# A norm by ScalarE's root, forms of one chunk made an expert later, and first products by pair of heads

## Chip, core and metric

The kernel runs on one core of one Trainium2 chip. The time is that of the whole program on the device, in microseconds (us); for this kernel the median of several executions is given. A core has five engines that run their own instruction streams in order and wait for each other by semaphores: TensorE (PE; its weight loads are listed apart as PEld), VectorE (DVE), ScalarE (ACT), GpSimd (POOL) and SyncE (SP), which here only issues DMA transfers. All data is float32.

## What is computed

Linear attention without softmax, normalised by its root mean square, followed by a mixture of four experts in which every token goes through every expert:

```python
# q, k, v: (8, 8, 576, 64); g_norm: (64,)
kv = np.einsum('bhsd,bhse->bhde', k, v)
out = np.einsum('bhsd,bhde->bhse', q, kv)
rms = np.sqrt(np.mean(out * out, axis=-1, keepdims=True) + 1e-06)
attn = out / rms * g_norm
x = attn.transpose(0, 2, 1, 3).reshape(4608, 512)
# domain_probs: (4608, 4); w1: (4, 512, 1024); w2: (4, 1024, 512)
p = domain_probs / (domain_probs.sum(-1, keepdims=True) + 1e-09)
for e in range(4):
    h = np.maximum(x @ w1[e], 0.0)
    out += p[:, e:e + 1] * (h @ w2[e])
```

## The kernel before

**Chunks.** The 4608 tokens are nine chunks of 512. Chunks 0 to 7 are the first 512 tokens of each batch element; chunk 8 holds the eight remainders of 64. The outer loop runs over the four experts, the inner one over the nine chunks; step s = 9e + c. Each step multiplies the chunk by w1 (`up`), applies relu, and multiplies by w2 (`down` or `down_deep`). Both products are made with fewer multiplications than usual: seven products of sums and differences of blocks (called forms, numbered 1 to 7, 12, 21) take the place of eight, and in `up` and `down_deep` this is done twice over, on quarters of blocks. The forms of the weights are made once for each expert (`weights_1`, `weights_2`), those of x once for each chunk (`x_forms`, in expert 0), stored to DRAM (`x_kept`), and loaded again for the later experts (`x_again`). Chunk 0 of expert 0 goes through `up_plain`, which needs no forms: eight output blocks i, each the sum of four products of a w1 block with x transposed, in two operations (dh = 0 and 1, each over two kt).

**Attention.** Batch element 0 is handled by `opening`, the others by `attention` in the steps of expert 0. In the opening each of four pairs of heads hp runs the same chain: `load_pair` issues loads of queries, keys and values (keys and values in 96 rows of 6 x 64 values, 1536 bytes in a run); `turn` transposes the queries on PE (L742); `key_values` multiplies keys by values (L761); `attend` multiplies queries by that (L788), into two PSUM banks `raw`; `scaled` squares on ACT (L640), sums on DVE (L647), computes (mean + 1e-6) to the power -0.5 on POOL in two instructions (L654, L658), and multiplies on DVE (L667); `turn_x` transposes on PE (L806), and ACT copies the result with the gains into half of x (L814; pairs 0 and 1 make the half xh[0], pairs 2 and 3 xh[1]). `attention` does the like for two pairs at once, with the power on POOL in L940 and L944, the multiply in L950 and the transposes in L1069.

**The order of the work** is made ahead by a planner (class `Plan`). Every operation has a key (steps of the program as a decimal number), estimated costs on the engines that may run it, the buffers that it reads and writes, and kinds of buffers with a fixed number of slots ("big" has 31, "xf" 5, PSUM banks "u1", "u2", "db", "ab" two each). The planner runs an event simulation with these costs: PE and SP take the first operation by key that is ready, the others the one that is due earliest, within a reach of about one key. An operation that names two engines (`either`) goes to DVE or POOL. The simulated order is the program order on every engine; estimates for transfers use the variables `bus` and `lanes`. While the first operation left on PE has a key under 0 and nothing is ready, the planner puts an `idle` operation on PE: two transposes of the identity into a free bank of "ab" or "db" (L1712), which compute nothing that is used. Operations marked `port` on DVE and POOL are kept from running at the same time by a dependency added at the end.

The helper `halves_of` records nearly all products (L410), `combine` all sums of forms (L433), `load` all loads (L439); one float32 matmul shows as two records on PE.

## Time and profile before

| | |
|---|---|
| median of 4 runs | 1666.7 us (1664.95 to 1668.14) |
| the profiled execution | 1665.69 us, span 1663.6 us |
| granted TensorE clock, mean | 0.999 |
| HBM read, written | 155.79 MB, 74.19 MB |

The span is from the first to the last instruction of the program. Times in the profile are from the span's start. Busy time of an engine is the union of its instructions; a matmul's end is modelled. Lines of the waits say which instruction's start waited for whom. A group's name such as `ab<-ident` is what the instruction writes and reads, by the program's names for buffers.

The stage that ends first is the opening with `up_plain` (about 0 to 60 us); the steps of expert 0 with attention go on to about 490 us, and each later step takes about 43 us.

| stretch, us | PE busy | DVE | ACT | POOL | DMA share, GB/s |
|---|---|---|---|---|---|
| 0 to 61.4 | 58.35 | 34.55 | 21.35 | 22.90 | 0.89, 221 |
| 150 to 194 (expert 0) | 44.00 | 34.40 | 25.35 | 26.75 | 0.69, 197 |
| 498 to 542 (expert 1, first step) | 44.00 | 36.26 | 29.14 | 25.21 | 0.67, 150 |
| 672 to 716 (expert 1) | 44.00 | 31.14 | 27.54 | 16.64 | 0.46, 112 |

### The profile page before, as it was taken

To read this page: it belongs to the slowest core of one execution; us is meant where nothing else is said; L and a number is where in the kernel's file an instruction comes from. 1 tells how busy PE (TensorE), PEld (TensorE's weight loads), DVE (VectorE), ACT (ScalarE), POOL (GpSimd) and SP (SyncE) were. 2 spreads that over 40 slices of the span, in tenths; PEclk is the share of its full clock that TensorE was granted. 3 is DMA by queue.
4 is the path that set the end of the run, shared out by engine and by line. 5 is a ranking of instruction groups with operands and counts; after the bars stand their busy time and mean duration, and the time that the engine had idled before them with its cause. 6 is when DMAs were issued, how large, how long until landed. Compare 5 with 4: busy or idle time off the path is not lost.

```text
span 1663.6 us, 66253 instructions
## 1 busy us (share of the span) xinstructions
PE 1651.4 (99%) x28884; PEld 1557.3 (94%) x28884; DVE 1250.8 (75%) x2051; ACT 972.8 (58%) x2391; POOL 705.0 (42%) x701
## 2 busy tenths in 40 slices
PE   9999999999999999999999999999999999999998
PEld 6587888888899999999999999999999999999996
DVE  4768777677788887776778777777788778777774
ACT  3355555555456666666666665656566566666662
POOL 3545443343445343333354554333355554333321
PEclk9999999999999999999999999999999999999999
DMA  9876765535456454444577444444579444444443
GB/s 220 196 224 189 214 177 148 143 124 182 149 172 147 125 121 114 113 109 115 144 177 177 116 119 114 110 109 116 133 179 200 116 116 116 104 115 116 116 104 52
DMA packets 208123, 234.27 MB, mean 141 GB/s; under 512 B 97368, under 2 KB 148440, under 8 KB 207832
## 3 DMA queue, kind: packets, MB, share of 16 engines
q1 hardware_dynamic: 184760, 193.32, 38.6%
q0 software_dynamic: 23072, 36.71, 15.5%
q8 instruction: 227, 3.72, 0.9%
q14 instruction: 64, 0.52, 0.1%
HBM read 155.79 MB, written 74.19 MB: 138 GB/s over the span
## 4 chain that ended last, share of the span: by engine, by line
PE 98%; DVE 1%; POOL 0%; DMA 0%; issue 0%; SPq 0%; ACT 0%; DVEq 0%; POOLq 0%; ACTq 0%
PE u L410 47%; PE db L410 32%; PE ab L410 15%; PE ab L1001 1%; PE ab L1069 1%; PE ab L1028 1%; PE ab L1712 1%; DMA big<-in_moe_w_dram 0%; DVE big L433 0%; PE ab L742 0%; POOL rt L944 0%; SPq L439 0%; PE ab L761 0%; PE ab L1090 0%; PE db L1037 0%
## 5 line engine op out<-in xcount | busy, mean ns | idle before, releaser
L433 DVE TENSOR_TENSOR big<-big,big 128x1024 f32<-128x1024 f32 (+1 forms) x527 | 518.7, 1001 | 35.7 <-ACT big L1226 15.9
L410 PE MATMUL u<-xf,big 128*64 128x128 f32 x6784 | 486.9, 273 | 0.2
L410 PEld LDWEIGHTS u<-xf,big 128*64 128x64 f32 x6784 | 394.0, 137 | 5.4 <-issue 1.0
L410 PE MATMUL u<-xf,w1y 128*64 128x128 f32 x5304 | 385.8, 273 | 0.0
L410 PE MATMUL db<-big,big 128*64 128x128 f32 (+1 forms) x4280 | 361.2, 308 | 1.3 <-ACT big L1576 0.4
L1270 DVE TENSOR_TENSOR big<-u,snap 128x256 f32<-128x256 f32 x476 | 199.5, 421 | 209.1 <-PE u L410 136.1
L433 POOL TENSOR_TENSOR big<-big,big 128x256 f32<-128x256 f32 (+1 forms) x196 | 219.1, 1135 | 224.6 <-DVE big L433 118.5
L410 PEld LDWEIGHTS u<-xf,w1y 128*64 128x64 f32 x5304 | 308.9, 137 | 2.4 <-issue 1.0
L410 PEld LDWEIGHTS db<-big,big 128*64 128x64 f32 x4280 | 262.3, 137 | 42.8 <-issue 2.8
L1262 ACT ACTIVATE snap<-u 128x256 f32<-128x256 f32 x490 | 188.2, 384 | 195.2 <-PE u L410 142.2
L1262 ACT ACTIVATE big<-u 128x256 f32<-128x256 f32 x476 | 181.7, 384 | 66.3 <-PE u L410 41.4
L1576 ACT ACTIVATE snap<-db 128x256 f32<-128x256 f32 (+1 forms) x230 | 82.4, 358 | 116.5 <-PE db L410 106.7
L1226 ACT ACTIVATE big<-big 128x1024 f32<-128x1024 f32 x134 | 140.7, 1050 | 5.6 <-DVE big L433 3.7
L433 POOL TENSOR_TENSOR big<-big 128x512 f32<-128x512 f32 (+1 forms) x76 | 94.4, 1250 | 114.9 <-DVE big L433 82.0
L410 PE MATMUL db<-small,big 128*64 128x128 f32 (+1 forms) x1552 | 116.9, 274 | 0.0
L1429 POOL DMA_DIRECT2D out_dram<-big x108 | 94.4, 1003 | 50.1 <-ACT big L1406 47.9
L1584 DVE TENSOR_TENSOR big<-ab,snap 128x256 f32<-128x256 f32 x166 | 69.9, 421 | 55.9 <-ACT snap L1576 30.0
L1262 ACT ACTIVATE u<-u 128x256 f32<-128x256 f32 x245 | 91.1, 372 | 24.5 <-PE u L410 9.1
L433 DVE TENSOR_TENSOR big<-big 128x512 f32<-128x512 f32 (+1 forms) x131 | 101.1, 784 | 1.8 <-PE u L410 1.7
L1614 POOL TENSOR_TENSOR big<-big 128x512 f32<-128x512 f32 x21 | 26.8, 1278 | 173.6 <-DVE big L433 140.9
L1406 ACT ACTIVATE big<-big,p_all 128x256 f32<-128x256 f32 x200 | 94.4, 501 | 5.4 <-POOL big L1614 4.0
L410 PEld LDWEIGHTS db<-small,big 128*64 128x64 f32 x1552 | 91.3, 137 | 0.7
(193 smaller groups left out, 2337.2 us busy)
## 6 DMA issues: line engine op xcount, KB each, us to landing
xf<-x SPq DMA_DIRECT2D x108, 512.0 KB, 3.7
out_dram<-big POOLq DMA_DIRECT2D x92, 256.0 KB, 5.5
xf<-x_h SPq DMA_DIRECT2D x81, 256.0 KB, 3.3
xf<-x SPq DMA_DIRECT2D x81, 256.0 KB, 3.7
x<-xf SPq DMA_DIRECT2D x36, 512.0 KB, 4.8
big<-in_moe_w_dram SPq DMA_DIRECT2D x32, 512.0 KB, 5.1
x_h<-big SPq DMA_DIRECT2D x18, 512.0 KB, 3.7
out_dram<-big SPq DMA_DIRECT2D x32, 256.0 KB, 3.6
```

The costliest lines, as they stand in the source:

```text
L410: nc.tensor.matmul(out_[cols], lhsT=lhsT[:, cols], rhs=rhs, **kw)
L433: lambda eng: adder(eng).tensor_tensor(out=out_(), in0=a(), in1=b(), op=op),
L1001: nc.tensor.matmul(bank.ap[r * D:(r + 1) * D, o * D:(o + 1) * D], lhsT=ks[r], rhs=vs[r], start=(j == 0), stop=(j == len(sets) - 1), skip_g ...
L1028: nc.tensor.matmul(raw[r].ap[c * D:(c + 1) * D, (o * NR + t) * D:(o * NR + t + 1) * D], lhsT=qt.ap[half, col:col + D], rhs=kv.ap[half, o * ...
L1226: lambda eng: nc.scalar.activation(out=b.ap[:], in_=b.ap[:], func=ACT.Relu),
L1262: lambda eng: nc.scalar.activation(out=where(), in_=ps.ap[:, 0:HN], func=ACT.Copy),
L1270: lambda eng: nc.vector.tensor_tensor(out=block(whole, a, t), in0=src.ap[:, 0:HN], in1=add_.ap[:], op=ALU.add),
L1406: lambda eng: nc.scalar.activation(out=cell(i, half), in_=ap(), func=ACT.Copy, scale=prob()),
L1429: nc.gpsimd.dma_start(out=dst, in_=cell(i)[parts, :], accum_op=ALU.add)
L1576: lambda eng: nc.scalar.activation(out=where(), in_=group_of(ps.ap), func=ACT.Copy),
L1584: lambda eng: nc.vector.tensor_tensor(out=cell(tq, dq), in0=group_of(src.ap), in1=group_of(add_.ap), op=ALU.add,),
L1614: lambda eng: adder(eng).tensor_tensor(out=whole(to), in0=whole(a), in1=whole(b), op=ALU.add),
```

## The change

Four things are changed, and some constants of the planner.

1. The power on POOL (`power`, in `scaled` and in `norm_rows` of `attention`) is replaced by `inverse_root`: ACT takes the square root of the mean plus epsilon, DVE takes its reciprocal r and makes one Newton step, r (1.5 - 0.5 a r r), with three more instructions.
2. The forms of chunk 0 are no longer made in expert 0. Only its two halves are stored. In expert 1 the chunk is taken fifth in place of first, and `x_first` loads its quarters, makes the forms and stores them for experts 2 and 3.
3. In `up_plain` a product is one operation for each pair of heads hp, which reads that pair's part of x (`x_part`), in place of one for each half. The first four blocks' products have keys under 0 for all four pairs. The opening's `raw` banks are halves of the two "db" banks for all pairs, so "u1" and "u2" stay free for the products; "db" is handed out when the opening's `raw` is done. The first block of w1 is loaded at key -2.85, behind the gains and before pair 2. The sums of w1's forms of expert 0 wait for the last norm of the opening (`after=opened`).
4. Keys and values are loaded in 72 rows of 8 x 64 values (2048 bytes in a run).

```diff
-        bus, port = 3.8, 0.0
+        bus, port = 2.5, 0.0
...
-                        bus = max(bus, t + 1.5) + op.kb / 215.0
-                        op.end = bus + 0.5
+                        bus = max(bus, t + 0.6) + op.kb / 215.0
+                        op.end = bus + 1.9
...
+    halved = slots["db"]
+    slots["raw"] = [[b[:, i * HN:(i + 1) * HN] for b in halved] for i in range(2)]
+    slots["db"] = []
     later = [
+        (("raw",), "db", halved),
...
-        return {"PE": passes * products * (0.0025 + columns / 1200.0) + 0.003}
+        return {"PE": passes * products * (0.0025 + columns / 1200.0)}
...
             load(
-                key + i * step, f[n],
+                key + i * step if e or i else -2.85, f[n],
                 lambda n=n: f[n].ap[:].rearrange("p (k u) -> p k u", k=2),
-                w1_src(e, dh, uh), 512 if e else 312, also=[corner[n]],
+                w1_src(e, dh, uh), 512 if e else 300, also=[corner[n]],
             )
...
-                [f[a], f[b], corner[a], corner[b]], [f[o], corner[o]],
+                [f[a], f[b], corner[a], corner[b]], [f[o], corner[o]], () if e else opened,
...
+    def inverse_root(key, ss, rt, n, count):
+
+        def root(eng):
+            nc.scalar.activation(
+                out=rt.ap[0:n, 0:count], in_=ss.ap[0:n, 0:count], func=ACT.Sqrt, scale=1.0 / D,
+                bias=eps[0:n, :],
+            )
+
+        def invert(eng):
+            a, r, w = ss.ap[0:n, 0:count], rt.ap[0:n, 0:count], rt.ap[0:n, 2 * H:2 * H + count]
+            nc.vector.reciprocal(out=r, in_=r)
+            nc.vector.scalar_tensor_tensor(
+                out=w, in0=a, scalar=D * EPS, in1=r, op0=ALU.add, op1=ALU.mult)
+            nc.vector.scalar_tensor_tensor(
+                out=w, in0=w, scalar=-0.5 / D, in1=r, op0=ALU.mult, op1=ALU.mult)
+            return nc.vector.scalar_tensor_tensor(
+                out=r, in0=w, scalar=1.5, in1=r, op0=ALU.add, op1=ALU.mult)
+
+        plan.add(key - 0.3, {"ACT": 0.2}, root, reads=[ss], writes=[rt])
+        plan.add(key - 0.3, {"DVE": 0.75}, invert, reads=[ss, rt], writes=[ss, rt], port=True)
...
-        plan.add(key - 0.3, {"POOL": 0.3 + 0.37 * blocks}, power, reads=[ss], writes=[ss, rt])
+        inverse_root(key, ss, rt, n, 2 * blocks)
...
-        splits = ((96, 6, 0),)
+        splits = ((72, 8, 0),)
...
-            kind = ("db", "u2", "u1", "db")[g]
-            raw = [Buf(kind, f"raw{n}_{r}") for r in range(2)]
+            raw = Buf("raw", f"raw{n}")
...
-                    reads=[bank, gains], parts=[xh],
-                )
+                    reads=[bank, gains], parts=[xh, x_part[hp]],
+                )
+        opened.append(turned)
...
-            plan.add(key - 0.3, {"POOL": 0.3 + 0.19 * count}, power, reads=[ss], writes=[ss, rt])
+            inverse_root(key, ss, rt, P, count)
...
+    def x_first(c, key, step):
+
+        views, f = {}, {m: Buf("xf", f"xf{c}_{m}") for m in OUTER}
+        base = {m: (lambda m=m: two(f[m].ap[:, 0:NT])) for m in OUTER}
+        from_half = {1: (0, 0), 2: (1, 0), 3: (1, 1), 5: (0, 1), 6: (1, 1), 7: (0, 1), 4: (1, 0)}
+        for j, m in enumerate(OUTER):
+            dh, th = from_half[m]
+            load(
+                key + j * step, f[m], base[m],
+                two(x_kept[c, f"h{dh}"][:])[:, :, th * HN:(th + 1) * HN], 256,
+                reads=[kept[c, f"h{dh}"]],
+            )
+        for m, a, b in ((5, 5, 1), (6, 6, 5), (7, 3, 7), (4, 4, 6)):
+            combine(
+                key + OUTER.index(m if m != 5 else 6) * step, either(NT), base[m], base[a], base[b],
+                ALU.subtract, [f[a], f[b]], [f[m]],
+            )
+        for j, m in enumerate(OUTER):
...
+            combine(
+                key + j * step, either(2 * P), lambda t=t: two(t.ap[:, NT:NT + 2 * P]),
...
+            for o, a, b in ((6, 3, 5), (4, 2, 6)):
+                combine(
+                    key + j * step, either(P), lambda block=block, o=at[o]: block(o),
...
+            keep(c, m, t, 256 if m in (1, 2, 3) else 512, key + j * step + 0.2, NT if m in (1, 2, 3) else 0)
+        return views
...
-            for dh in range(2):
+            for hp in range(NPAIR):
+                dh, kt = divmod(hp, 2)
                 w, low = corners[uh, dh]
 
-                def product(eng, w=w, bank=bank, dh=dh, ut=2 * a + u):
-                    for kt in range(2):
-                        halves_of(
-                            bank.ap[:], two(w.ap[:])[:, kt, ut * P:(ut + 1) * P],
-                            rhs=two(xh[dh].ap[:])[:, kt, :], start=(dh == kt == 0),
-                            stop=(dh == kt == 1), skip_group_check=True,
-                        )
+                def product(eng, w=w, bank=bank, dh=dh, kt=kt, ut=2 * a + u):
+                    halves_of(
+                        bank.ap[:], two(w.ap[:])[:, kt, ut * P:(ut + 1) * P],
+                        rhs=two(xh[dh].ap[:])[:, kt, :], start=(dh == kt == 0),
+                        stop=(dh == kt == 1), skip_group_check=True,
+                    )
 
                 op = plan.add(
-                    key - 0.89 + 0.01 * (i ^ 2) if i < 4 and dh == 0 else key + span * i / 8,
-                    pe(2, NT), product,
-                    reads=[w, low, xh[dh]], **({"parts": [bank]} if dh else {"writes": [bank]}),
+                    key - 0.89 + 0.04 * hp + 0.01 * (i ^ 2) if i < 4 else key + span * i / 8,
+                    pe(1, NT), product, reads=[w, low, x_part[hp]], holds=[xh[dh]],
+                    **({"parts": [bank]} if hp else {"writes": [bank]}),
                 )
...
-    x_forms(0, 0.45)
+    for dh in range(2):
+        keep(0, f"h{dh}", x_halves(0)[dh], 512, 1.35)
...
+    CHUNKS = {e: list(range(NCH)) for e in range(E)}
+    CHUNKS[1].insert(4, CHUNKS[1].pop(0))
...
-                    x_views[s + 1] = x_again((c + 1) % NCH, s + (0.05 if e else 0.6), 0.13)
+                    again = CHUNKS[(s + 1) // NCH][(s + 1) % NCH]
+                    made = x_first if (s + 1) // NCH == 1 and again == 0 else x_again
+                    x_views[s + 1] = made(again, s + (0.05 if e else 0.6), 0.13)
```

The planner's estimates also change for the first loads (queries 172 to 222 KB, keys and values 241 to 180), the later queries (140 to 115), keys and values (205 and 53 in place of 240 and 48), w2 of expert 0 (512 to 300), and for the products of keys and values (0.73 to 0.95 a pair in the opening, 1.42 to 1.2 for two pairs later) and of queries (1.45 to 1.33). The constant tile `mhalf` goes, `eps` comes; the tile "rt" is twice as wide.

## The prediction

> **What bounds the kernel.** I read the busy shares first. TensorE leads, and from about 65 us on it has hardly a gap, so a change can win only where TensorE does no needed work.
>
> ```profile
> span 1663.6 us, 66253 instructions
> ...
> PE 1651.4 (99%) x28884; PEld 1557.3 (94%) x28884; DVE 1250.8 (75%) x2051; ACT 972.8 (58%) x2391; POOL 705.0 (42%) x701
> ...
> PE ab L1069 <- DVE ss L933: 2.5, 1, 2.5
> ...
> PE ab L761 <- issue: 1.1, 1, 1.1
> PE ab L1069 <- DVE small L950: 0.8, 1, 0.8
> ```
>
> The last three lines are from the list of PE's waits (total, times, longest), where no wait but the first shown is over 1.4 us. But 99% hides filler: until the plan's key 0 the planner puts `idle` transposes (L1712) wherever PE has nothing ready. The chain of waits in order of time shows them as work:
>
> ```profile
> 1.35 3.49 PE ab L1712 x18
> ...
> 5.87 1.24 PE ab L1712 x10
> 7.11 0.85 PE ab L761 x24
> ...
> 21.71 1.20 PE ab L1712 x9
> 22.91 1.87 PE u L410 x8
> 24.78 0.59 PE ab L806 x4
> 25.37 1.87 PE u L410 x8
> 27.24 0.59 PE ab L806 x4
> 27.82 8.73 PE u L410 x40
> ```
>
> L410 at 22.91 is the first product of the experts; after it PE has no filler. Before it the chain has filler of 3.49 + 1.24 + 0.59 + 0.81 + 0.37 + 0.59 + 0.44 + 0.54 + 1.20 = 9.27 us and idle time of 1.35 + 1.07 + 0.29 = 2.71 us: 11.98 us without needed work. That is the first thing to win. The second is at 61 us, by the windows (PE, PEld, DVE, ACT, POOL busy; granted clock; DMA share; GB/s) and the timeline of PE and POOL:
>
> ```profile
> 61.40:65.00 3.60, 1.15 (x8) 0.84 (x8) 3.12 (x5) 0.93 (x2) 2.20 (x2) 1.00 0.94 215
> 65.00:70.00 5.00, 5.00 (x31) 2.98 (x32) 3.89 (x7) 0.83 (x2) 4.79 (x3) 0.66 0.71 116
> ...
> 63.85 1.25 PE L1069 MATMUL ab<-ident,small 128*128 128x128 f32 x8 [2.48 <-DVE ss L933]
> ...
> 58.06 3.75 POOL L944 TENSOR_TENSOR rt<-ss,mhalf 128x16 f32<-128x16 f32 x1
> ```
>
> PE waits 2.48 us for the norm of chunk 1, and in the next 5 us the granted clock is 0.66, which loses 0.34 x 5 = 1.7 us more. The price of that stop is 4.2 us. The remaining stops after 65 us come to about 2 us, and the end, behind the last product, is untouched.
>
> **Part 1, products by pair of heads, the first w1 block earlier.** Before, the first product reads all of x's first half (pairs 0 and 1) and w1. Pair 0's turned x is copied at 17.83 to 18.52 and pair 1's at 20.91 to 21.60 (ACT's timeline), and the four w1 loads are issued on SP from 10.16 on and take 9.6 us at the median. After, pair 0's x alone opens four products of 0.93 us (half of the 1.87 us of eight records), 3.7 us a pair, and one w1 block stands on SP's queue behind pair 1's loads; pairs 2 and 3 and every load behind them land one such block later. 512 KB at the 267 to 270 GB/s of the windows 5:10 and 10:15 is 1.9 us.
>
> When is pair 0's x ready? Its attend ends at 9.46, the squares at 10.17, the sum at 10.89. Before, POOL's scale and power follow (10.98 to 12.95), then DVE multiplies at 13.89, late because pair 1's sum (13.29) stands before it on DVE; PE turns the result only at 17.36, behind pair 2's keys, whose value load came late. After: 10.89 + root 0.25 + four small DVE operations 0.8 + multiply 0.76 + turn 0.5 + copy 0.69 + 0.5 for the six hand-overs (0.03 to 0.1 us each in the rows) = 14.4 us. From 4.85 (first queries landed) to 14.4 PE has 9.55 us, in which it does three query turns (1.02 + 0.88 + 0.88), two key products at 1.13, two attends at 0.62 and one turn at 0.44: 6.7 us; 2.8 us stays filler. From 14.4 on it always has something: products of pairs 0 to 2 are 11.2 us and the remaining opening steps about 6 us, to 31.6, while pair 3's x is ready at about 25.4 (its values landed by 17.4, where its key products start at 17.79; 1.4 to 1.9 later now; then the same chain of some 6.5 us). So time without needed work falls from 11.98 to 4.85 + 2.8 = 7.65: **4.3 us won**. Lower bound 1.5, if x of pair 0 is turned only at 17.2 as now; upper bound 5.5, if half of the 2.8 also goes.
>
> **Part 2, 2 KB loads of keys.** A load is cut 72 x 8 in place of 96 x 6. For PE that is 32 records for 24 a pair: 0.85 x 32/24 = 1.13, four times +0.28 = **1.1 us lost**, since PE is now the bound there. For DMA it is fewer, longer packets at equal bytes. The trace has no 72-row load; the w1 loads, with 2 KB rows, run in the window 15:20 at 363 GB/s, against 273 and 269 in 5:10 and 10:15. Bounds: a pair's 576 KB of keys and values take 2.2 us at 270, 1.6 at 363, and 3.1 at the 187 GB/s of the window 25:30 with its short rows; so pair 0's x comes 0.6 earlier or 0.9 later. I take 0: the same queries, with their 1 KB rows, stay in the mix that ran at 270.
> The Trainium skill ("DMA: Bandwidth & Descriptors", section "Why a DMA increments its semaphore by 16 and not by 1") speaks against this edit: a transfer is spread over the largest number up to 16 that divides its slowest dimension, so 96 rows use 16 engines and 72 only 12. By that a pair's 576 KB of keys and values over 12 engines and 256 KB over 16 would take (48 + 16)/52 = 1.23 times as long, an estimate from the page; pair 0's x would be ready about 0.8 us later, and the sum's first term would be 3.5. No view here shows the engines of one load.
>
> **Part 3, the norm.** Five power calls in the opening (1.64 us each, plus 0.20) and 21 in `attention` (median 2.9, longest 3.76) leave POOL. Each becomes one ACT root, bounded by the 64-column copy of 0.22 and the 128-column one of 0.28, and DVE's reciprocal and three small operations: 4 x 0.18 by L465 to 0.38 + 3 x 0.30 by L466 and L464; 0.8 taken. 26 x 0.8 = 21 us of DVE in the 480 us of expert 0, where a stretch of 43 has about 33 busy: hidden by 10 us of slack in each. Behind them on DVE stand the multiplies that wait for them anyway. At 61 us: the sum of chunk 1's norm ended at 53.05, but POOL took it at 56.91, behind a w2 form (54.47, 2.36 us) that waited for a load. After: 53.05 + 0.25 + 0.8 + 1.23 = 55.3 on free engines, against 63.07 now, and PE, 3 us earlier, wants it at 58. The stop goes: **4.2 us won**. Lower bound 1.75, see rival A. The second stop of this kind (L1069 on L950) gives **0.8**, bounds 0 to 0.8.
> Does the root need another activation table? The page has one ACT_TABLE_LOAD, 1.28 us, for Copy, Square and Relu together. One more at the first root would run while DVE sums (0.69): 0.6 us late, once; I take 0, and 0.6 as the bound.
> The Trainium skill ("ScalarE: Activation LUTs", section "Table sets: the hidden batching unit") says to batch activations by set, and that a root among other sets' functions pays 2.66 us for each switch, though cheap functions sit in every set. If the squares or copies weren't in the root's set, 26 roots would cost 52 switches, 138 us of ACT by the page; if they are, one switch.
>
> **Part 4, chunk 0's forms in expert 1.** Expert 0 loses four 128x512 and seven sets of 256 + 2 x 128 columns: 4 x 0.7 + 7 x (0.41 + 2 x 0.28) = 9.6 us of DVE or POOL between 33 and 52 us and seven stores (2.8 MB) after. Nothing on PE's path waits for them except chunk 1's w1 and w2 forms behind them on DVE, so at most it secures part 3. Expert 1 gains the same 9.6 us, seven 256 KB loads for ten of 3.5 MB in all, and seven stores on SP. Cover there, in the windows of a quiet stretch:
>
> ```profile
> 629.00:672.00 43.00, 43.00 (x793) 43.00 (x790) 32.96 (x50) 26.80 (x68) 15.89 (x16) 1.00 0.45 113
> ```
>
> DVE 32.96 + 9.6 = 42.6 of 43 if POOL took none; POOL has 27 us free, DMA half. Priced 0; if the cover fails, one stop like that at 61 us, 4.2. w1's forms now wait for the last norm (about 24 us), as they in fact did (23.69 and 24.43); their user is 45 us away. The new plan constants only reorder; I price them 0, with 1.5 us either way.
>
> **Sum.** 4.3 - 1.1 + 4.2 + 0.8 = 8.2 us off the profiled execution's 1665.7 (span 1663.6 plus 2.1 around it): 1657.5. The four runs' median is 1.0 higher, so 1658.5.
>
> **Rivals.**
> A. DVE takes POOL's place at 61 us. The root's DVE steps can queue behind the w2 forms, which wait for loads landing there (DVE runs them 55.80 to 59.04 and 59.60 to 60.83). Then the multiply ends at 62.1 instead of 63.07, PE, 3.2 us early, waits 4 us, and the opening's gain and the clock's loss both go there: only 1.75 and the 0.8 remain, 1664. For it: both engines work in order. Against: the plan can put the multiply before the forms, as the sums are 2.7 us earlier on DVE.
> B. The opening doesn't shorten: the turn of pair 0 stays behind pair 2's keys, or loads come later, and 1.5 - 1.1 = 0.4 is won there; with 4.2 to 5.0 later, 1662. Each half is as likely.
> C. Slower: tables are switched around each root. The place is ACT in expert 0, the price two loads of 1.28 us for each of 26 norms, 67 us of ACT; the banks `u1` and `u2` are only two each, so PE would lose at least the part that its 0.4 us of cover leaves: some 26 x 1 to 2 us, less the 8.2: 1685 to 1710. It decides when Square or Relu isn't in the table that has the root. Against: one table now holds all three.
> D. The plan's new order, or expert 1's DVE, makes two new stops of 4.2 us each that eat the gain: 1667, no change.
>
> **Chances.** 0.2% is 3.3 us, about what this kernel's measurements can tell from no change. Main case 0.55 (1654 to 1662.5), A 0.13, B 0.14, C 0.06, D 0.12. Faster: the main case, most of B, and a third of A: 0.72. Same: the rest of A and B and half of D: 0.17. Slower: C and some of D: 0.11. The range for 8 in 10 is 1654 to 1667: below, both upper bounds and 1.5 from the plan; above, up to D.
>
> **What would show it.** PE's first L410 at 14 to 15 us, less than 8 us of filler and idle time before it; L761 at 1.1 us a pair; no stop at L1069 and no granted clock under 0.9 near 60 us; no `mhalf` on POOL, and one or two table loads; PE busy 43 of 43 in expert 1. I am wrong if the first product is near 18 or later, if L1069 stops behind DVE's L433, or if table loads number over 20.

## The result and the profile after

| | before | after |
|---|---|---|
| median, us | 1666.08 (1664.17 to 1668.21, 55 runs) | 1669.10 (1666.30 to 1671.51, 35 runs) |
| ratio after / before | | 1.0017, 95% interval 1.0012 to 1.0022 |
| span of the profiled execution, us | 1663.6 | 1667.6 |
| mean granted TensorE clock over the executions | 0.9992 | 0.9974 |

The change makes the kernel 0.17% slower: inside the 0.2% that was called no change, but on the other side from the forecast and above its range. The last row says part of it already. A clock of 0.9974 over 1664 us is a loss of up to 4.3 us, one of 0.9992 of up to 1.3. These are upper bounds, since a low clock costs nothing while PE waits; in the profile of after PE works in 8.5 of the 10.2 us at half clock.

The page's first lines, and the list of PE's waits (total, times, longest), of after:

```profile
span 1667.6 us, 66400 instructions
...
PE 1652.5 (99%) x28894; PEld 1559.0 (93%) x28894; DVE 1271.0 (76%) x2141; ACT 979.2 (59%) x2421; POOL 661.6 (40%) x660
```

```profile
PE ab L1015 <- DMA kv<-in_v_dram: 3.5, 2, 2.0
PE ab L780 <- DMA big<-in_v_dram: 2.5, 2, 2.1
...
PE u L414 <- ACT snap L1316: 0.8, 1, 0.8
PE ab L1015 <- ACT small L932: 0.6, 1, 0.6
```

The stop that was to go is gone: the transposes of chunk 1 (L1069 before, L1083 now) wait for nothing. In its place two waits for transfers stand at the top: L1015 multiplies keys by values of chunk 1, L780 those of the opening. Before, none of the ten longest entries was a wait for a DMA. The chain of waits of after, in order of time (start, length):

```profile
7.49 9.07 DMA big<-in_v_dram
...
16.70 1.20 PE ab L780 x32
17.90 1.16 PE ab L761 x16
...
19.68 0.85 PE ab L827 x4
...
23.35 1.01 PE u L414 x4
...
39.89 0.68 SPq L459
40.61 2.39 SPq L459
43.05 1.29 SPq L459
...
48.75 5.30 DMA kv<-in_v_dram
54.19 1.34 PE ab L1015 x20
```

Two things are read from it. First the opening: pair 2's keys (L780) start at 16.70 behind a load of values issued at 7.49, pair 0's x is turned (L827) only at 19.68, behind them, and the first product (L414) starts at 23.35, against 22.91 before. Second, the chain that sets the end now runs through SP: seven loads of the probabilities (L454 to L462, issued from 38.87 to 45.66) stand on SP ahead of chunk 1's second set of keys and values, whose last long load is issued at 48.75 and lands 5.30 us later, and the short one behind it at 54.26; PE has asked for the set since 49.7. The windows of after show the price (columns as before the change: the engines' busy time, granted clock, DMA share, GB/s):

```profile
15.00:20.00 5.00, 3.30 (x53) 3.00 (x54) 1.70 (x8) 1.12 (x3) 0.00 (x0) 0.84 1.05 245
20.00:25.00 5.00, 5.00 (x109) 3.44 (x108) 1.71 (x6) 2.56 (x6) 2.19 (x3) 0.82 0.83 216
44.00:48.00 4.00, 4.00 (x22) 1.40 (x20) 0.48 (x2) 0.89 (x3) 2.71 (x4) 1.00 0.41 50
50.00:55.00 5.00, 1.82 (x35) 1.64 (x37) 1.15 (x5) 0.20 (x1) 2.09 (x3) 0.75 1.11 262
55.00:60.00 5.00, 5.00 (x53) 2.08 (x53) 3.22 (x3) 0.75 (x2) 0.00 (x0) 0.57 1.05 239
```

From 50 to 55 us PE is busy 1.82 of 5.00 us, and the clock falls to 0.75 and 0.57: in the clock's records 6.83 us at half speed from 52.5 us on, of which PE works 5.1, so 2.6 us are lost. Another 3.41 us at half speed begin at 18.4, after the wait of 2.1 us at L780: 1.7 us lost. In the two profiled executions PE ends 3.8 us later. Its idle time grew by 2.7 us (7.8 to 10.5), the loss by the clock by 2.6 (1.7 to 4.3), the key products by 0.9 (0.92 to 1.15 a pair in the timelines); filler fell by 2.3 (9.2 to 6.9). That makes 3.9 of the 3.8.

A second measure is used below: how much later than before a kernel's PE reaches the same amount of product work, from the starts of all product records, each weighed at full clock. After stands at +0.5 us at 30 us, +6.6 at 50 us, +4.5 at 67 us (before has its own stop and half clock in between), +4.4 at 490 us and +3.8 at the end. All of the loss is made in the first 60 us. Expert 1, with chunk 0's forms, adds 0.4 us, within what comes and goes elsewhere.

### The profile page after: what moved, and what is told of

It is laid out like the page before. It is cut to its first block, busy times and chain, and to the rows that moved or that the text cites. A ratio compares the mean times of both kernels' runs of the same rounds, so it can differ in the third digit from the quotient of the medians.

```text
span 1667.6 us, 66400 instructions
## 1 busy us (share of the span) xinstructions
PE 1652.5 (99%) x28894; PEld 1559.0 (93%) x28894; DVE 1271.0 (76%) x2141; ACT 979.2 (59%) x2421; POOL 661.6 (40%) x660
## 4 chain that ended last, share of the span: by engine, by line
PE 97%; DMA 1%; SPq 1%; ACT 0%; issue 0%; DVE 0%; ACTq 0%; DVEq 0%
PE u L414 47%; PE db L414 32%; PE ab L414 15%; PE ab L1015 1%; PE ab L1042 1%; PE ab L1083 1%; DMA big<-in_v_dram 1%; DMA big<-in_q_dram 0%; DMA kv<-in_v_dram 0%; SPq L459 0%; SPq L443 0%; PE db L1051 0%; PE ab L827 0%; PE ab L1104 0%; PE ab L780 0%
## 5 line engine op out<-in xcount | busy, mean ns | idle before, releaser
L437 DVE TENSOR_TENSOR big<-big,big 128x1024 f32<-128x1024 f32 (+1 forms) x506 | 483.6, 969 | 39.1 <-ACT big L1280 13.0
L414 PE MATMUL u<-xf,big 128*64 128x128 f32 x6784 | 487.2, 273 | 0.8 <-ACT snap L1316 0.8
L414 PEld LDWEIGHTS u<-xf,big 128*64 128x64 f32 x6784 | 393.8, 137 | 5.3 <-ACT snap L1316 1.3
L414 PE MATMUL u<-xf,w1y 128*64 128x128 f32 x5304 | 384.7, 273 | 0.2 <-DVE big L1324 0.2
L414 PE MATMUL db<-big,big 128*64 128x128 f32 (+1 forms) x4424 | 367.4, 306 | 1.5 <-issue 1.1
L1324 DVE TENSOR_TENSOR big<-u,snap 128x256 f32<-128x256 f32 x456 | 190.7, 421 | 183.8 <-PE u L414 136.8
L414 PEld LDWEIGHTS u<-xf,w1y 128*64 128x64 f32 x5304 | 308.5, 137 | 3.5 <-issue 0.8
L414 PEld LDWEIGHTS db<-big,big 128*64 128x64 f32 x4424 | 270.4, 137 | 42.0 <-issue 2.6
L1316 ACT ACTIVATE big<-u 128x256 f32<-128x256 f32 x456 | 174.3, 384 | 87.8 <-PE u L414 65.0
L437 POOL TENSOR_TENSOR big<-big 128x512 f32<-128x512 f32 (+1 forms) x82 | 101.1, 1233 | 135.8 <-DVE big L437 99.0
L1483 POOL DMA_DIRECT2D out_dram<-big x100 | 89.2, 1135 | 46.0 <-ACT big L1460 36.9
L414 PE MATMUL db<-small,big 128*64 128x128 f32 (+1 forms) x1304 | 98.1, 274 | 0.0
L414 PE MATMUL ab<-big,big 128*64 128x128 f32 (+1 forms) x1368 | 95.2, 276 | 0.0
L414 PE MATMUL db<-kv,big 128*64 128x128 f32 x1280 | 88.2, 273 | 0.0
```

What stands on the lines that cost most here:

```text
L414: nc.tensor.matmul(out_[cols], lhsT=lhsT[:, cols], rhs=rhs, **kw)
L437: lambda eng: adder(eng).tensor_tensor(out=out_(), in0=a(), in1=b(), op=op),
L1316: lambda eng: nc.scalar.activation(out=where(), in_=ps.ap[:, 0:HN], func=ACT.Copy),
L1324: lambda eng: nc.vector.tensor_tensor(out=block(whole, a, t), in0=src.ap[:, 0:HN], in1=add_.ap[:], op=ALU.add),
L1483: nc.gpsimd.dma_start(out=dst, in_=cell(i)[parts, :], accum_op=ALU.add)
```

## The experiments

Each was executed 5 to 11 times, with the kernel before on the same chip beside it; the ratio is to that, with its 95% interval. "Lead" is the measure above in the profiled execution against the profile of before, negative when earlier; profiled executions scatter by up to 2.5 us about a kernel's median, so verdicts go by medians and ratios.

| run | median, us | ratio | lead at 30, 67 us, end |
|---|---|---|---|
| after | 1669.10 | 1.0017 (1.0012 to 1.0022) | +0.5, +4.5, +3.8 |
| e1 after, 96 rows | 1666.78 | 1.0001 (0.9992 to 1.0010) | -0.7, +5.0, +2.7 |
| e2 before, 72 rows | 1668.33 | 1.0012 (1.0003 to 1.0021) | +1.1, +3.5, +3.5 |
| e3 after, no probabilities | 1662.55 | 0.9978 (0.9968 to 0.9987) | +1.5, -0.7, -2.4 |
| e4 after, 96 rows, none | 1662.93 | 0.9975 (0.9964 to 0.9986) | -1.5, -2.7, -5.0 |
| e5 after, 96 rows, issued by POOL | 1664.31 | 0.9993 (0.9984 to 1.0002) | -1.9, +3.2, +0.9 |
| e6 before, no probabilities | 1664.16 | 0.9988 (0.9979 to 0.9997) | +1.3, -1.8, -1.2 |
| e7 before, norm alone | 1666.80 | 1.0002 (0.9993 to 1.0011) | -0.1, -0.5, +2.1 |
| e8 after, old estimates | 1672.65 | 1.0040 (1.0027 to 1.0052) | +2.4, -0.5, +8.3 |
| e9 after, turn first | 1669.54 | 1.0019 (1.0010 to 1.0028) | -0.8, +6.0, +4.0 |
| e10 turn and root first | 1668.84 | 1.0016 (1.0007 to 1.0025) | +0.2, +5.7, +3.5 |
| e11 after, probabilities later | 1667.42 | 1.0007 (0.9998 to 1.0016) | -1.0, +2.4, +0.1 |
| e12 e10 and e11, 96 rows | 1665.96 | 0.9997 (0.9988 to 1.0007) | -1.7, +0.2, -2.1 |
| e13 after, wide loads | 1668.02 | 1.0011 (1.0002 to 1.0020) | +0.4, +4.8, +2.5 |
| e14 before, wide loads | 1666.34 | 1.0001 (0.9992 to 1.0010) | -0.4, +1.1, +0.6 |
| e15 e10, 96 rows, wide loads | 1666.34 | 1.0002 (0.9992 to 1.0011) | -1.6, +3.8, +1.5 |
| e16 after, wide loads by POOL | 1663.48 | 0.9988 (0.9979 to 0.9997) | +0.2, +2.8, +0.5 |
| e17 e10, 96 rows, wide by POOL | 1661.21 | 0.9974 (0.9963 to 0.9985) | -2.1, -2.1, -4.4 |
| e18 e10, 96 rows, none | 1660.93 | 0.9971 (0.9962 to 0.9981) | -1.8, -2.5, -4.8 |

### The rows of keys and values: e1, e2

e1 is after with the old rows and the same order of work on every engine; e2 is before with the new rows.

```diff
-        splits = ((72, 8, 0),)
+        splits = ((96, 6, 0),)
```

> The kernel after with keys and values of the opening loaded in 96 rows of 6 x 64 again; the planner's figures are kept, so the order on every engine is the same. Theory T (a 72-row load is spread over 12 of 16 DMA engines and the whole opening's transfers run late): pair 2's values land at 14 to 15 us in place of 16.6, the last w1 block at 22.5 to 24 in place of 26.4, the 2.1 us stop of PE at L780 is under 0.6, the first product starts at 20.5 to 22, and the time falls by 3 to 7 us to 1662 to 1666. Rival R (the w1 block ahead of pair 2 is what makes pair 2 late, the rows are harmless): pair 2's values still land after 16, the stop stays over 1.5, and only the 1.1 us of fewer key products are won: 1667.5 to 1668.5.

> The kernel before with keys and values of the opening loaded in 72 rows of 8 x 64; the order on every engine is that of before. Theory T: each pair lands 0.3 to 0.7 us later than the pair before it did, the last w1 block 2.5 to 4 us later (25 to 27 in place of 22.7), the first product 2 to 4 us later than 22.9, and the time rises by 2 to 5 us to 1668 to 1671. Rival R: landings within 0.5 us of before, the four longer key products lie under filler, and the time is within 1 us of before.

Both ways the 72 rows cost about 2 us: 2.3 in after, 1.9 in before. In before, the first product comes 1.1 us later with them (24.02 for 22.91) and the last w1 load lands at 26.67 in place of 22.70. The trace's records of semaphore updates show why: a load of 72 rows has 13 updates, one some 0.6 us after its issue (1.84 us for a load issued at 1.25) and twelve at its end (4.67 to 5.15), a load of 96 or of 128 rows has 16. The Trainium skill ("DMA: Bandwidth & Descriptors", section "Why a DMA increments its semaphore by 16 and not by 1") has a transfer spread over the largest number of engines up to 16 that divides its slowest dimension, which is 12 for 72 rows; the twelve updates agree. The stop at L1015 stayed in e1 (5.2 us in its profile), so the rows are not its cause. Pair 2's values landed at 16.75 even so, behind something else (last section).

### The probabilities taken out: e3, e4, e6

In these three the seven loads of the probabilities are left out and the probabilities are ones; the rest is computed and the order is the same.

```diff
+        nc.gpsimd.memset(p_all[:], 1.0)
         def load_all(eng):
-            nc.sync.dma_start(...)
+            return None
```

> The kernel after without the seven loads of the expert probabilities (the weights of the experts are all set to one in their place, so they are left out of the result); same order elsewhere. Theory T2 (the stops of 1.4 and 2.0 us at L1015 come because these loads hold SP's queue from 38.9 to 45.7, with the next keys and values behind them): keys and values are issued from about 39.5, PE has no stop over 0.5 us between 45 and 60, no granted clock under 0.9 there, and the time falls by 4 to 7 us to 1662 to 1665. Rival R2 (they are late by the opening's lateness of the transfers alone): the stops stay within 1 us of what they are and the time moves by less than 1.5 us.

> Both edits together (96 rows, and no loads of probabilities, which are left out of the result). Theory T with T2: gains add up in part, since the 96 rows also bring the keys and values earlier: 1658 to 1662. If R and R2 hold: 1666 to 1668. If only one cause is real, the time equals that of the one edit within 1.5 us.

> The kernel before without the loads of the probabilities (all experts weighted by one; left out of the result), same order elsewhere. Theory V1 (only the new order is hurt by these loads): within 1.5 us of before, 1665 to 1667.5, and the stop of 2.5 us at L1069 stays. Theory V2 (in before they make the w2 loads late in the same way, POOL's form waits for those, and the power behind it makes the stop at 61 us): w2's second pair lands before 52, the stop at L1069 is under 0.5, and the time falls by 3 to 5 us to 1661.5 to 1663.5. By V2 the whole change is worth nothing once the loads are out of the way; by V1 it is worth about 3 us.

The loads of the probabilities cost after 6.5 us and before 1.9. Without them PE's waits in e3 begin so:

```profile
PE ab L780 <- DMA big<-in_v_dram: 2.9, 2, 1.5
...
PE u L414 <- ACT snap L1316: 0.8, 1, 0.8
```

L1015 no longer waits for a DMA, and there is no half clock between the first product and the end. e3 against e6 is the change without these loads: 1662.55 to 1664.16, 1.6 us faster by the medians. The intervals of the two ratios overlap by a little, so that the change brings something there is likely and not shown; with the loads it is 3.0 us slower. In e6 before loses its own stop too: the wait at L1069 falls from 2.5 to 0.6 us and no half clock follows, as POOL's w2 form starts 1.1 us earlier (53.38 for 54.47) and PE comes later; only 1.9 us of that reach the median, with a wait of 1.0 us at L1090 among what takes the rest. So both kernels pay for the same seven loads, in different places. In e4 the rows made no further difference to the median, though its profile is 2.6 us ahead of e3's: what they cost showed only in the runs with these loads.

### The same loads from another queue: e5

After with 96 rows, and `nc.gpsimd.dma_start` for `nc.sync.dma_start` in the seven loads.

> The kernel after with 96 rows, and with the seven loads of the expert probabilities issued from POOL in place of SP; the order of everything else is the same. If the price of these loads is that they hold SP's queue for 6.9 us before the next keys and values: PE's stops at L1015 fall from 5.2 us (with 96 rows) to under 1.5, no clock under 0.9 at 50 to 60, and the time is near that without the loads, 1662 to 1664.5. If it is the time of their many small packets on the DMA engines: the stops stay over 3 us and the time at 1666 to 1668. A third way: POOL holds back the sums of forms behind the seven issues, and PE stops elsewhere before 60 us by 2 us or more.

2.5 us faster than e1, but the stop stayed (4.9 us). SP now issued chunk 1's second set from 39.95 on, 5.8 us earlier than in after, and yet it landed from 48.8 to 53.1, little earlier. Between 36 and 42 us the DMA engines are at a full share and move only 81 to 128 GB/s; the queries' packets of 128 bytes took 34 ns each on average, for 16 in e1, and landed 3.3 us later. So SP's time is not the only price. How the small loads hold the engines the trace doesn't show: in this run it lists them as 112 packets of 256 to 896 bytes, which take little time themselves.

### The norm alone, and the old estimates: e7, e8

e7 is before with `inverse_root` in both places and nothing else, planned anew; e8 is after with all estimates of the planner as before.

```diff
-        bus, port = 2.5, 0.0
+        bus, port = 3.8, 0.0
...
-                        bus = max(bus, t + 0.6) + op.kb / 215.0
-                        op.end = bus + 1.9
+                        bus = max(bus, t + 1.5) + op.kb / 215.0
+                        op.end = bus + 0.5
```

> The kernel before with the norm alone changed (ACT's root and DVE's Newton step in place of POOL's power), planned anew. If the norm is what the prediction took it for: no stop at L1069 at 61 us and no half clock there, 3 to 5 us won, 1661.5 to 1663.5, with at most two table loads. If another wait takes its place (the keys' and values' loads, or w2's forms on DVE): a stop of 1.5 us or more with a named releaser between 45 and 70, and 1665 to 1668.

> The kernel after with the planner's figures of before (start of the transfers, their latency, sizes of loads, times of products), planned anew; all that is executed stays as after but for the order. Theory P1 (the new figures believe transfers early, and so PE's order has the second set of keys and values too soon): L1015's second set stands later in PE's order, the stops there are under 1 us, the time 1663 to 1666. Theory P2 (the order is set by the finer products, not by the figures): the stops stay over 2.5 us and the time is within 1.5 us of after, 1667.5 to 1670.5.

e7 removes the stop at L1069 and its half clock, as forecast, and is no faster: PE waits 1.4 us for ACT at 62.3 in its place, and, ahead by 1.3 us at 175 us, the run is 2.1 behind at the end. Three stops of 0.4 to 0.6 us near the starts of experts (565.8, 848.5, 1234.8 us) make 1.5 of that; the rest was not located. They come with the new order, where the norm itself no longer runs. e8 is 3.6 us slower than after: its wait for keys at L1015 is only 0.9 us, but it has stops at 63.5, 94, 127 and 129.6 us and 6.83 us of half clock there. The estimates decide which stops an order has, and the new ones were not the harm; either order has its own stops.

### Pair 0's turn first, the root first: e9, e10

After with a piece of its order altered by hand; in e10 also one root of a single column as ScalarE's first instruction, and the two products ahead of pair 2's keys.

```diff
+    turned, copied = find("xT0_0"), find("x0_0")
+    turned.outs[0].slot, turned.outs[0].ap = 1, slots["ab"][1]
+    moved = [copied, keys_2, copy_2, turn_3, copy_3, attend_2, find("up0_2"), find("up0_3")]
+    for op in moved:
+        order.remove(op)
+    at = order.index(turned) + 1
+    order[at:at] = moved
...
         nc.vector.memset(eps[:], EPS)
+        nc.scalar.activation(out=tot[:, 0:1], in_=eps[:], func=ACT.Sqrt)
```

> The changed kernel with one piece of its order altered by hand: the turn of pair 0's x, and the copy behind it, stand ahead of pair 2's keys on PE and ACT, and pair 2's attend and two of pair 0's products follow the queries of pair 3; the two filler transposes that stood before the turn fall into the wait for pair 2's values. Theory (the order keeps pair 0's turn behind keys that land at 16.6 us, and the table load makes its x ready only at 15.7): the turn starts at 15.7 inside the idle time of 14.6 to 16.7, the first product at 19.5 to 20 in place of 23.3, but only the 0.8 us of the turn and 0.5 us of filler are saved; the time is 1.0 to 1.5 us under the changed kernel's 1669.1. Rival (pair 0's place alone cost the whole opening term of the prediction): the time falls by 3 us or more.

> As the run before, with two products of pair 0 ahead of pair 2's keys, and with one root of a single column as ScalarE's first instruction, so that only one table is loaded, at 0.7 us. Theory: one ACT_TABLE_LOAD in the profile, pair 0's x ready at 14.4 (1.28 us earlier), turn at 14.4, first product at 15.9 to 16.2, 2 to 3 us in all under the changed kernel; so 0.7 to 1.5 us under the run before, which is what the second table load costs. Rival (the table load is hidden, as the prediction had it): no difference from the run before.

In e9 the first product moves from 23.3 to 19.2 us, and the work at 30 us is done 1.3 us earlier than in after, both as expected. The time does not move. The timeline of PE of e9 says where the 1.3 us went:

```profile
51.74 1.55 PE L1015 MATMUL ab<-kv 120*64 120x64 f32 x20 [3.34 <-DMA kv<-in_v_dram]
55.20 1.34 PE L1015 MATMUL ab<-kv 120*64 120x64 f32 x20 [1.90 <-DMA kv<-in_v_dram]
```

PE comes earlier and waits 5.2 us in place of 3.5 for the same transfers, and the half clock behind it costs 4.0 us in place of 2.6 (10.24 us long, with PE at work in 7.9). In e10 the table is loaded once, at 0.74 us, and the first product comes at 16.8, 6.5 us before that of after. But a first product is not work saved: it changed places with work that has to be done too. By 30 us e10 is only 0.3 us ahead of after, since PE stops 1.06 us in an attend without a releaser and 0.71 for pair 3's values. The expected 0.7 to 1.5 us against e9 did not show (0.7, with intervals that overlap); the price of the second table load is below what can be told.

### The loads later on SP: e11, e12

e11 is after with the seven loads behind the two w2 loads that follow chunk 1's second keys and values; e12 adds e10 and 96 rows.

```diff
+    load_p, norm_p = find("probs", "load_all"), find("probs", "norm")
+    for op, behind in ((load_p, find("w2_0_3")), (norm_p, find("q1_0", n=-1))):
+        order.remove(op)
+        order.insert(order.index(behind) + 1, op)
```

> The changed kernel with the seven loads of the probabilities moved on SP from before chunk 1's second set of keys and values to behind them and the two w2 loads that follow, and their norm on DVE moved behind chunk 1's norm. Nothing is left out and no other engine's order changes. Theory (PE waits at 49 to 54 us because those keys and values stand behind 6.9 us of small loads): keys and values land some 7 us earlier, no stop at L1015 over 0.8 us and no granted clock under 0.9 at 50 to 60 us, 5 to 6.5 us under the changed kernel: 1662.6 to 1664. Rival (the stop moves to whatever stands behind the small loads now, the keys of chunk 2 or the forms of w2): 0 to 3 us.

> All of it together: probabilities later, root first, pair 0's turn and two products first, and keys and values in 96 rows. Theory: 1669.1 less 5 to 6.5 for the probabilities, 2 to 3 for the opening's order and table, 0 to 2.3 for the rows: 1658 to 1662, faster than both kernels. Rival: the gains are the same gap counted twice, as the kernel without probabilities was no faster in 96 rows than in 72 (1662.9 and 1662.6): 1662 to 1664.

The rival was right: chunk 1's stop falls to 1.1 us, and 2.67 us with a half clock appear at 64.1, at the keys of chunk 2, which now stand behind the loads. 1.7 us won of 5 to 6.5 expected. e12, at 1665.96, had the same stop (2.58 at 62.0) and no more than the kernel before.

### Fewer and longer packets: e13, e14, e15

The probabilities come as 32 tokens of four values in a run of 512 bytes, 256 packets for 4224 in all (the 3712 below was miscounted), nine loads for seven, and are put in place by four 32x32 block transposes on DVE.

```diff
+            rows = moe_domain_probs.rearrange("(b n c) e -> b n c e", b=B, c=32)
+            for g in range(4):
+                nc.sync.dma_start(
+                    out=p_all[32 * g:32 * g + 28, NR:, :], in_=rows[1:, g:16:4, :, :])
+                nc.sync.dma_start(
+                    out=p_all[32 * g + 28:32 * g + 32, NR:, :],
+                    in_=rows[g // 2::2, 16 + g % 2, :, :])
...
+            for i in range(E):
+                nc.vector.transpose(out=p_all[:, NR:, i], in_=p_all[:, NR:, i])
```

> The changed kernel with the probabilities loaded in runs of 512 bytes (32 tokens of four values) in place of 16, in nine loads with 256 packets for seven with 3712, turned into place by four 32x32 block transposes on DVE ahead of their norm; nothing is left out, and no other engine's order changes. Theory (PE is held at 49 to 54 us by transfers, of which the 16-byte packets take some 3 us of all DMA engines, and their issue 6.9 us of SP): issue 5 us, no stretch at under 30 GB/s near 45 us, the stop at L1015 under 1.5 us with no half clock behind it, 1662.5 to 1664.5, near the 1662.55 of the kernel without these loads. Rival (the place of the loads on SP counts, not their packets): the stop stays within 1 us of 3.5 and the time over 1667.

> The kernel before with the same edit alone. Theory: the kernel before has the same bottleneck in a milder form, 1664 to 1665.5, as the 1664.16 without the loads; the change is then worth 1 to 2 us with this edit on both sides. Rival: no difference, 1666.

> The changed kernel with the wide loads of the probabilities in their old place, 96 rows, root first, and pair 0's turn and two products first. Theory (the opening's gains are given back only because PE waits for transfers at 49 to 65 us): with that wait shortened the opening's 2 us stay, 1660 to 1662, faster than both kernels by more than 0.2%. Rival (another transfer ends the wait, chunk 2's keys and values at 60 to 64): 1662.5 to 1665, no better than the run with the wide loads alone.

The theory failed, the stop stayed (3.9 us), and before gained nothing. One window of e13 shows the reason:

```profile
44.00:48.00 4.00, 4.00 (x22) 1.31 (x20) 0.25 (x2) 0.79 (x3) 3.47 (x5) 1.00 0.05 13
```

The DMA engines stand idle (share 0.05, against 0.41 in after's window of the same time) while SP is still at the nine loads, from 39.35 to 46.5 us. Issuing takes 5.6 us of that, against 6.5 for after's seven; the 0.9 us saved went into a wait of 1.2 us on SP for a load of w2, which landed at 45.20. Chunk 1's second set is issued at 46.61 and lands up to 54.4. Small packets and SP's queue each hold the transfers back, so taking one away shows little: 1.1 us here, 2.5 in e5.

### Both: e16, e17, e18

The wide loads with `nc.gpsimd.dma_start`: e16 after with nothing else, e17 with 96 rows and e10's opening, e18 that opening and 96 rows without the loads (probabilities of one, as in e4).

> The changed kernel with the wide loads of the probabilities issued from POOL's queue, at the same place in the order; nothing else is altered and nothing left out. Theory (both halves count: the small packets hold the DMA engines for some 4 us, as the run with POOL's issue of them showed, and nine or seven issues hold SP for 7 us, as the run with wide loads on SP showed with the engines at a share of 0.05 meanwhile): SP reaches chunk 1's second keys and values at 39 to 40, they land by 49, the stop at L1015 is under 1 us with no half clock, 1662.5 to 1664. Rival (POOL's issue costs its forms, which PE then waits for, or the transfers are late for a third reason): over 1666.

> The same with 96 rows, the root as ScalarE's first instruction, and pair 0's turn and two products ahead of pair 2's keys. Theory: the stop gone, the opening's gain stays: 1659 to 1662, faster than the kernel before by over 0.2%. Rival: an earlier PE meets chunk 1's or chunk 2's transfers again, 1662.5 to 1665.

> The same opening and 96 rows without the loads of the probabilities, which are ones here, as in the run of the changed kernel with 96 rows and without these loads (1662.93): the only difference from that run is the opening's order and the table. Theory: with nothing to wait for at 49 to 54 us the opening's gain stays, 1.5 to 3 us less, 1660 to 1661.5. Rival (transfers bound the stretch even without these loads): 1662.5 to 1663.5.

e16 is 5.6 us faster than after by the medians (4.8 by the ratios, as the kernel before differs a little between the sets) and 0.12% under before, with the whole change in it. In its profile the same window reads

```profile
44.00:48.00 4.00, 4.00 (x22) 1.37 (x20) 3.86 (x12) 0.66 (x2) 1.42 (x2) 1.00 1.10 235
```

and SP issues chunk 1's second set from 40.72 on, 5.0 us earlier than after. A wait of 3.1 us was left in the profiled execution, with one half clock, and the set landed at 53.3, only 1 us earlier than in after; so the expected stop of under 1 us was not reached, though the time was. This execution was 2.5 us above e16's median; none nearer to it was profiled. The Trainium skill ("Perfetto Trace Analysis", section "DMA Optimizations") advises to batch small transfers and, where descriptor generation is the bottleneck, to balance DMAs over SP, ScalarE and GpSimd; here each alone gave 1 to 2.5 us (the second with 96 rows, e5 against e1), both some 5.

e17 leaves nothing out and is the fastest full version: 1661.21 us, ratio 0.9974 (0.9963 to 0.9985), 4.9 us under before and 7.9 under after by the medians. Its timeline of PE at the same place:

```profile
47.31 0.80 PE L1015 MATMUL ab<-kv 120*64 120x64 f32 x20 [0.16 <-DMA kv<-in_v_dram]
49.96 0.80 PE L1015 MATMUL ab<-kv 120*64 120x64 f32 x20 [1.85 <-DMA kv<-in_v_dram]
```

A wait of 1.85 us is left, with no half clock behind it. Against e16 it wins 2.3 us, as much as the rows alone did in e1, though the intervals of the two ratios overlap. e18 against e4, which differ in the opening alone, is 0.9971 to 0.9975: no difference that can be told. Both still wait at L1015, 1.0 us in e4 and 1.5 in e18. So with the stop mostly gone the opening's new order brings 0.7 us by the ratios, within their error, and its part of e17 is not shown.

## Why the prediction was wrong, point by point

**Planner constants "only reorder; I price them 0".** This step failed, and with it the choice of the main case over rival D. Rival D named it (the plan's new order makes new stops that eat the gain, 1667) and got 0.12. The stop is 3.5 us at L1015, and the half clock behind it costs 2.6 more. What was left out is a margin that stood in the trace of before: the last of chunk 1's second set of loads landed there at 52.4 us and L1001 started on it at 52.88, so PE's need had 0.5 us of slack on a transfer. PE's timelines show what the new order did to it, of before:

```profile
47.54 1.16 PE L1028 MATMUL ab<-kv,small 64*64 64x64 f32 x64
...
50.72 0.46 PE L866 MATMUL ab<-ident,big 64*128 64x64 f32 x4
51.11 1.94 PE L410 MATMUL u<-big,big 128*64 128x512 f32 x8
52.88 1.34 PE L1001 MATMUL ab<-kv 120*64 120x64 f32 x40
```

and of after:

```profile
51.14 1.01 PE L1015 MATMUL ab<-kv 120*64 120x64 f32 x20 [1.43 <-DMA kv<-in_v_dram]
...
59.53 1.16 PE L1042 MATMUL ab<-kv,small 64*64 64x64 f32 x64
```

In before these keys stand behind 112 records of the expert's products with 512 columns, chunk 1's first attend (L1028) and a turn (L866). In after they stand behind 100 of the records, with the attend and the turn still to come. By before's times that is 4.4 us of work moved from ahead of the need to behind it (2.7, 1.3 and 0.4). PE was no faster: the hundredth record ends at 49.9 in before and at 49.7 in after, where the attend is still to come. In before's order after's PE would have come to these keys at about 54.1 (an estimate, 49.7 + 4.4), about when they landed. SP's queue read the same way: loads of the probabilities from 37.05 to 44.14 and those keys behind them in before, and in after the keys at 45.75, 1.6 us later, so the load lands 1.9 us later (54.3). So PE asks 3.2 us earlier, by the order alone, and the load comes later. e8, with the old estimates, has the need back behind 124 records, at 58.55 us without a wait, and other stops instead; before's order of this piece alone, with the rest of after, was not run. That the loads ahead of them make the stop, e3, e9, e11 and e16 show from four sides: without the probabilities the time falls by 6.5 us, an earlier opening adds its lead to this wait, with the probabilities behind them it falls to 1.1 us, and the loads made cheap in both ways give about 5 us back.

**Part 1, 4.3 us won.** Filler and idle time before the first product fell by 1.2 us (11.9 to 10.8: 6.9 of filler and 3.9 idle), not by 4.3; the key products' 0.9 and the half clock at 18.4 took that back, and after is 0.5 us behind at 30 us. The failing step is "x ready at 14.4": DVE's multiplies of pair 0 ended at 15.67, since the table load was not hidden and pair 1's sum (14.33) went ahead of them, the very place seen in before. Worse, the plan kept the turn behind pair 2's keys, as rival B had it, and those came later: their values landed at 16.57 in place of 13.11. One w1 block was put ahead of them, which landed at 11.56 and was first used at 23.35; pair 2's queries, next behind it, came 2.1 us later (12.75 for 10.69), so it explains some 2 of the 3.5 us. No run took the block back. e9 undid the place and e10 the table; neither moved the time.

**Part 2, 1.1 us lost on PE, DMA taken as 0.** PE's part is right in the main (1.15 for 0.92 us a pair in the timelines, 0.9 in all). The DMA part, taken as 0, was mis-sized: with it the rows cost 1.9 to 2.3. The sum by the page (1.1 + 0.8 = 1.9) was the better one.

**Part 3, 4.2 and 0.8 us won.** The mechanism is right: the stop and its half clock at 61 us are gone in after and in e7, DVE's four small operations take 0.8 us (0.24 + 0.18 + 0.17 + 0.17 at the median), rival A did not occur. The gain didn't reach the time: in e7, with the norm alone, other stops took it, and e6 loses most of the same stop with POOL's power kept. The table load, priced 0 with 0.6 as bound, is exposed by 1.28 us, for it stands behind pair 1's copy on ACT, later than the sum. The 2.66 us a switch that the prediction quotes did not show: from the copy's end at 11.60 to the root at 12.92 are 1.32 us. ACT's timeline of after:

```profile
11.38 0.22 ACT L793 ACTIVATE kv<-ab 128x64 f32<-128x64 f32 x1 [0.89 <-PE ab L780]
11.63 1.28 ACT L632 ACT_TABLE_LOAD   x1
12.92 0.30 ACT L632 ACTIVATE rt<-ss,eps 128x8 f32<-128x8 f32 x1
```

**Rival C** did not occur: there are two table loads in the whole trace, with 26 roots.

**Part 4, priced 0.** Right: PE is busy 43 of 43 us in expert 1 (629 to 672 us), and the lag grows by 0.4 us from 490 to 590; it shrinks by 0.6 until 1300 us and by 0.4 at the end.

**The sum.** Of 8.2 us expected, e3 against e6 has 1.6 where the loads of the probabilities are out of the way. Part 3's stop is small in e6 to begin with (0.6 us, no half clock), so most of its 4.2 us can't show in that pair. Of the rest some 3 us in the opening and 1 in the rows were never there.

## What to carry to other kernels

Before counting a gain, look ahead of it for the next transfer that the bounding engine needs: the time from its landing to the first use is all that an earlier first use can win, and an engine that is at 99% hides that. A new order moves such a need as a faster engine does: list what stands ahead of each load's first use before and after. A load's date depends on the queue that issues it as well as on the bytes; here taking away one of the two brought 1 to 2.5 us, and both some 5. An earlier first product is no measure of a faster opening; compare when a fixed amount of the work is done.

## What was not expected of the hardware

**Half clock in steps.** Every interval of lower clock in these traces, but for the last one of each, is 3.41 us long or a multiple (6.83, 10.24), at 0.5, and begins in or up to 1.8 us behind a stop of PE of 1.6 us or more, or two stops near each other (1.38 and 1.68 us in e16). The Trainium skill ("TensorE: Matmul & The Clock Gate", section "What's actually happening") gives a free-running window of 3413 ns, and the lengths agree. Whether a stop of this size brings one varies: e17's 1.85 us and e1's 1.98 at 16.9 brought none, e8's 1.61 one. So a stop cost its length plus half of what PE worked in the interval: here nothing, 1.6 to 1.7 us of 3.41, 2.5 to 3.3 of 6.83 and 4.0 of 10.24.

**Long packets among the loads.** The queue named "instruction" moves packets of 16 KB that take 0.9 to 1.6 us each, some six of them in the first 70 us. The load in flight lands later: pair 3's keys in before at 16.17, 2.2 us behind the queries ahead of them, where the other pairs' keys came 1.1 us behind, with such a packet at 12.35 us; pair 2's values in e1 at 16.75 with one at 13.80. Which load is hit differs between kernels and executions, perhaps one reason for the scatter. That it is the cause was read from the times and not tried.

**Issue time on SP.** A load of the probabilities took SP 0.43 to 2.39 us to issue with 16-byte runs (up to 896 packets in a load) and 0.46 to 0.91 with 512-byte ones (4 or 28 packets). With two loads more the shorter lists saved 0.9 us of issue in all, which the wait for w2 took back (e13).
